# Moving the last LN1 tile, the reciprocal's spread and the later LN2 tiles in a fused attention and mixer kernel

## The chip, the core and the metric

The kernel runs on one core of one Trainium2 chip. A core has five engines that run at the same time and meet through semaphores: TensorE (PE in the profile; its weight loads are PEld), VectorE (DVE), ScalarE (ACT), GpSimd (POOL) and SyncE (SP), which in this kernel issues nearly all the transfers. Each engine takes its instructions in program order. The kernel fixes that order itself ("manual schedule"), so moving a line of Python moves an instruction in the queue of its engine.

The metric is device time in microseconds of the one core. The kernel before takes 265.07 us, the median of three runs (264.65 to 265.18). The profiled execution spans 264.0 us.

## The reference, cut to what matters

The input `x` has 2048 rows of 640 columns. Two branches are computed from it and mixed by a gate, row by row.

```python
g = sigmoid((x * gate_w).sum(-1))                 # one gate per row
# branch A: linear attention, 32 heads of 20 columns
q, k, v = split(x @ wqkv);  pq, pk = phi(q), phi(k)   # phi: t + 1 where t > 0, else exp(t), plus 1e-6
num = pq @ (pk^T v)                               # per head
den = pq . sum_over_rows(pk) + 1e-6               # one per row and head
a = (num / den) @ wo
# branch B: mixer and MLP
h  = gelu(layernorm(x) @ w1)                      # LN1
hs = row_shifted(h) @ w2                          # column groups shifted by +-1, +-2 rows
x1 = x + hs
b  = x1 + gelu(layernorm(x1) @ w3) @ w4           # LN2
out = g * a + (1 - g) * b
```

## The kernel before: the parts concerned

The 2048 rows are four tiles `t` of 512 rows, each of four chunks `cc` of 128 rows. `pair()` hands out one of four PSUM buffers in turn, each of two banks. `work` has four buffers for a normalized chunk `ln`, and `lnx_p` three for a transposed tile `lnxT`.

LayerNorm is applied on DVE and the result is transposed by a DMA, since the next product needs it with the columns on the partitions. LN1 of a chunk and LN2 of a chunk look alike; LN2 needs `x1`, which needs the product with `w2`:

```python
def ln1_apply(c):
    ...
    nc.vector.tensor_scalar(lnx[:], x_sb[:, c, 0:D], mv1[:, c, 0:1], rstd1[:, c:c + 1], ...)
    nc.sync.dma_start_transpose(lnxT[t][:, :, cc * P:(cc + 1) * P], lnx[:])

def w2_unit(t, cc):
    pt = pair()
    ...  # 10 matmuls
    nc.vector.tensor_tensor(x1, pt, x_sb, op=ALU.add)      # L431, frees the PSUM buffer
    ln_stats(...)                                           # two bn_stats, one bn_aggr (L290 to L292)

def ln2_apply(t, cc):
    ...
    nc.vector.tensor_scalar(ln[:], x1, mean, rstd, ...)     # L445; rstd is made on POOL (L286, L287)
    nc.sync.dma_start_transpose(st[t]["lnT"][:, :, cc * P:(cc + 1) * P], ln[:])   # L447
```

The denominators of the attention come out of PSUM, are inverted and spread over four tiles; four DMAs then copy them to the partitions where `pqT` has its rows, and `scale_t` multiplies `pqT` by them:

```python
def den_evac(pt):
    nc.vector.tensor_scalar_add(d, pt[:, 0, :], 1e-6)       # L265
    nc.vector.reciprocal(r_bf[:], d)                        # L267
    for t in range(NT):
        nc.vector.tensor_copy(r4[:, t, :], r_bf[H * t:H * (t + 1), :])   # L269
    for i in range(4):
        nc.sync.dma_start(rb[bass.ds(i, H, 4), :, :], r4[:])             # L271

def scale_t(t):                                             # L275
    nc.vector.tensor_tensor(pqT tile t, pqT tile t, rb[:, t] broadcast, op=ALU.mult)
```

The order in which the units are emitted, from the first product with `w1` on (each call adds its instructions to the queues of its engines at that place):

```python
for fcs in w1_split: w1_unit(0, fcs)          # w1_unit(t, (4,)) also makes four DVE copies of hx (L360)
kv_unit()
w1_unit(1, w1_split[0])
den_evac(den_mm())
for g in range(3): m_unit(g)
for cc in range(CPT): ln1_apply(3 * CPT + cc)
w1_unit(1, w1_split[1]); m_unit(3); m_unit(4); w1_unit(1, w1_split[2]); m_unit(5)
...
for cc in range(CPT):                         # tile 0: LN2 chunk by chunk
    w2_unit(0, cc)
    ln2_rstd(0, cc, cc + 1)
    if cc >= 1: ln2_apply(0, cc - 1)
for fcs in w1_split:
    w1_unit(2, fcs)
    if fcs[0] == 0: ln2_apply(0, CPT - 1)
m_regroup()                                   # mst to DRAM (2 DMAs, L389), back as m_sb (6 DMAs, L393)
load w4                                       # L576 to L578, 2.2 MB
scale_t(0); scale_t(1)
for fcs in w1_split: w1_unit(3, fcs)
scale_t(2); scale_t(3)
for cc in range(CPT): x1_scale(0, cc)
for t in range(NT):                           # the main loop
    for i in range(NW3):                      # NW3 = 7
        w3_unit(t, i)                         # 10 matmuls (5 for i = 6), L475, read the transposed LN2 tile t
        if i < CPT and t + 1 < NT: w2_unit(t + 1, i)        # L428
        if 2 <= i < 2 + CPT: att_unit(t, i - 2)             # 10 matmuls L459; DVE L462 adds into x1
    if t + 1 < NT:
        ln2_rstd(t + 1, 0, CPT)
        for cc in range(CPT): ln2_apply(t + 1, cc)
    if t == 0: w3_rest(0, ...)
    w4_tile(t)   # 52 matmuls L508, 8 matmuls L517, w3_rest(t + 1): 10 matmuls L483, 52 matmuls L508
```

`w3_rest(t + 1)` (L483) multiplies the last 64 columns of `w3` with the transposed LN2 tile `t + 1`. It is the first reader of that tile.

Of the kernel before, what the change touches and what calls it, by code (L numbers as in the profile page):

```python
# [16 lines left out]
def kernel(  # L17
# [20 lines left out]
    NT = S // TS  # L38
    CPT = TS // P
# [31 lines left out]
    def pair():  # L71
        return ps.tile([P, 2, 512], F32, name="pp")
# [182 lines left out]
    def den_mm():  # L255
        pt = pair()
        for j in range(DC):
            for t in range(NT):
                nc.tensor.matmul(pt[32 * t:32 * (t + 1), 0, :], lhsT=zbd[:, j, :], rhs=pqT[:, j, t * TS:(t + 1) * TS],
                                 start=(j == 0), stop=(j == DC - 1))  # L260
        return pt

    def den_evac(pt):
        d = e_p.tile([P, 1024], BF16, name="e")[:].bitcast(F32)
        nc.vector.tensor_scalar_add(d, pt[:, 0, :], 1e-6)  # L265
        with nc.allow_low_precision(reason="rounded after a float32 division, as a copy would"):
            nc.vector.reciprocal(r_bf[:], d)  # L267
        for t in range(NT):
            nc.vector.tensor_copy(r4[:, t, :], r_bf[H * t:H * (t + 1), :])  # L269
        for i in range(4):  # L270
            nc.sync.dma_start(rb[bass.ds(i, H, 4), :, :], r4[:])  # L271
# [13 lines left out]
    def rsqrt(out_ap, var_ap):  # L285
        nc.gpsimd.tensor_scalar_add(out_ap, var_ap, EPS)  # L286
        nc.gpsimd.tensor_tensor(out_ap, out_ap, mhalf[:, 0:out_ap.shape[1]], op=ALU.pow)  # L287

    def ln_stats(mv_ap, src_ap, st):
        nc.vector.bn_stats(st[:, 0, :], src_ap[:, 0:HD])  # L290
        nc.vector.bn_stats(st[:, 1, :], src_ap[:, HD:D])
        nc.vector.bn_aggr(mv_ap, st)  # L292
# [8 lines left out]
    def ln1_apply(c):  # L301
        t, cc = divmod(c, CPT)
        if cc == 0:
            lnxT[t] = lnx_p.tile([P, DC, TS], BF16, name="lnxT")
        lnx = work.tile([P, D], BF16, name="ln")
        nc.vector.tensor_scalar(lnx[:], x_sb[:, c, 0:D], mv1[:, c, 0:1], rstd1[:, c:c + 1],
                                op0=ALU.subtract, op1=ALU.mult)
        nc.sync.dma_start_transpose(lnxT[t][:, :, cc * P:(cc + 1) * P], lnx[:])
# [36 lines left out]
    def w1_unit(t, fcs):  # L345
        pt = pair()
        for i, fc in enumerate(fcs):
            for dc in range(DC):
                w = w1_sb[:, dc, CG * fc:CG * fc + P] if fc < 4 else w1x[:, dc, :]
                nc.tensor.matmul(pt[:, i, :], lhsT=w, rhs=lnxT[t][:, dc, :], start=(dc == 0), stop=(dc == DC - 1))  # L350
        for i, fc in enumerate(fcs):
            if fc < 4:
                o = 2 + shifts[fc] + t * TS
                nc.scalar.activation(hsT[:, fc, o:o + TS], pt[:, i, :], ACT.Gelu_apprx_tanh)
            else:
                hx = hx_p.tile([P, TS], BF16, name="hx")
                nc.scalar.activation(hx[:], pt[:, i, :], ACT.Gelu_apprx_tanh)
                for g in range(4):
                    o = 2 + shifts[g] + t * TS
                    nc.vector.tensor_copy(hsT[32 * g:32 * (g + 1), 4, o:o + TS], hx[32 * g:32 * (g + 1), :])  # L360
# [19 lines left out]
    def m_unit(g):  # L380
        pt = pair()
        for hf in range(2):
            nc.tensor.matmul(pt[:, hf, 0:HD], lhsT=kvT[:, row0[g]:row0[g] + P],  # L383
                             rhs=wo_sb[:, g, hf * HD:(hf + 1) * HD], start=True, stop=True)
        nc.scalar.copy(mst[:, g, :].rearrange("p (h e) -> p h e", h=2), pt[:, :, 0:HD])

    def m_regroup():
        for g in (0, 3):
            nc.sync.dma_start(m_dram[g:g + 3].rearrange("g p e -> p g e"), mst[:, g:g + 3, :])  # L389
        for g in range(NG):  # L390
            n = 4 * heads[g]
            p0 = P - DC * n if g == 5 else 0
            nc.sync.dma_start(m_sb[4 * head0[g]:4 * head0[g] + n, :, :],  # L393
                              m_dram[g, p0:p0 + DC * n, :].rearrange("(j r) e -> r j e", j=DC))
# [4 lines left out]
        w1_unit(0, fcs)  # L399
    kv_unit()  # L400
    w1_unit(1, w1_split[0])
    den_evac(den_mm())
    for g in range(3):
        m_unit(g)
    for cc in range(CPT):
        ln1_apply(3 * CPT + cc)
    w1_unit(1, w1_split[1])
    for g in range(3, 5):
        m_unit(g)
    w1_unit(1, w1_split[2])  # L410
    m_unit(5)
    s1.close()
    w4p = ctx.enter_context(tc.tile_pool(name="w4p", bufs=1))
    w4_sb = w4p.tile([P, FF + 1, D], BF16)
# [6 lines left out]
    def w2_unit(t, cc):  # L421
        c = t * CPT + cc
        if cc == 0:
            st[t] = dict(x1=[], mv=small.tile([P, CPT, 2], F32, name="mv2"))
        pt = pair()
        for hf in range(2):
            for fc in range(DC):
                nc.tensor.matmul(pt[:, hf, 0:HD], lhsT=hsT[:, fc, 2 + c * P:2 + (c + 1) * P],  # L428
                                 rhs=w2_sb[:, fc, hf * HD:(hf + 1) * HD], start=(fc == 0), stop=(fc == DC - 1))
        x1 = x1p.tile([P, D], F32, name="x1")  # L430
        nc.vector.tensor_tensor(x1[:].rearrange("p (h e) -> p h e", h=2), pt[:, :, 0:HD],  # L431
                                x_sb[:, c, 0:D].rearrange("p (h e) -> p h e", h=2), op=ALU.add)
        ln_stats(st[t]["mv"][:, cc, :], x1[:], small.tile([P, 2, 6], F32, name="bnst")[:])
        st[t]["x1"].append(x1)

    def ln2_rstd(t, c0, c1):
        if c0 == 0:
            st[t]["rstd"] = small.tile([P, CPT], F32, name="rstd2")
        rsqrt(st[t]["rstd"][:, c0:c1], st[t]["mv"][:, c0:c1, 1])

    def ln2_apply(t, cc):
        if cc == 0:
            st[t]["lnT"] = lnx_p.tile([P, DC, TS], BF16, name="lnxT")
        ln = work.tile([P, D], BF16, name="ln")
        nc.vector.tensor_scalar(ln[:], st[t]["x1"][cc][:], st[t]["mv"][:, cc, 0:1], st[t]["rstd"][:, cc:cc + 1],  # L445
                                op0=ALU.subtract, op1=ALU.mult)
        nc.sync.dma_start_transpose(st[t]["lnT"][:, :, cc * P:(cc + 1) * P], ln[:])  # L447
# [6 lines left out]
    def att_unit(t, cc):  # L454
        c = t * CPT + cc
        pt = pair()
        for hf in range(2):
            for j in range(DC):
                nc.tensor.matmul(pt[:, hf, 0:HD], lhsT=pqT[:, j, c * P:(c + 1) * P],  # L459
                                 rhs=m_sb[:, j, hf * HD:(hf + 1) * HD], start=(j == 0), stop=(j == DC - 1))  # L460
        x1 = st[t]["x1"][cc][:].rearrange("p (h e) -> p h e", h=2)
        nc.vector.scalar_tensor_tensor(x1, pt[:, :, 0:HD], gate[:, c:c + 1], x1, op0=ALU.mult, op1=ALU.add)  # L462
# [3 lines left out]
    def w3_unit(t, i):  # L466
        if i == 0:
            st[t]["h2"] = h2p.tile([P, FF * TS], BF16, name="h2")
        h2, lnT = st[t]["h2"], st[t]["lnT"]
        pt = pair()  # L470
        n = min(2, FF - 2 * i)
        for k in range(n):
            fc = 2 * i + k
            for dc in range(DC):
                nc.tensor.matmul(pt[:, k, :], lhsT=w3_sb[:, dc, fc * P:(fc + 1) * P], rhs=lnT[:, dc, :],  # L475
                                 start=(dc == 0), stop=(dc == DC - 1))
        nc.scalar.activation(h2[:, 2 * i * TS:(2 * i + n) * TS], pt[:].rearrange("p h e -> p (h e)")[:, 0:n * TS],  # L477
                             ACT.Gelu_apprx_tanh)
# [92 lines left out]
    for fcs in w1_split:  # L571
        w1_unit(2, fcs)
        if fcs[0] == 0:
            ln2_apply(0, CPT - 1)
    m_regroup()
    nc.sync.dma_start(w4_sb[:, 0:FF, :], B_w4[0:FF * P, :].rearrange("(c p) f -> p c f", p=P))  # L576
    nc.sync.dma_start(w4_sb[0:FR, FF, :], B_w4[FF * P:F, :])
    nc.sync.dma_start(w4_sb[FR:P, FF, :], B_w4[FF * P:F, :])  # L578
# [9 lines left out]
    for t in range(NT):  # L588
        for i in range(NW3):
            w3_unit(t, i)  # L590
            if i < CPT and t + 1 < NT:
                w2_unit(t + 1, i)
            if 2 <= i < 2 + CPT:
                att_unit(t, i - 2)
        if t + 1 < NT:
            ln2_rstd(t + 1, 0, CPT)
            for cc in range(CPT):
                ln2_apply(t + 1, cc)
        if t == 0:
            w3_rest(0, pair()[:, 0, 0:LT])  # L600
        w4_tile(t)
# [30 lines left out]
```

## Time and profile before

| engine | busy us | share of the span |
|---|---|---|
| PE (matmul) | 258.5 | 98% |
| PEld (weight load) | 159.1 | 60% |
| DVE | 142.4 | 54% |
| ACT | 83.2 | 32% |
| POOL | 18.5 | 7% |

A matmul on 512 columns is listed with a mean of 379 ns (L475); since matmuls overlap, ten of them take 2.16 us in the chain of work. The page also counts 1670 matmuls and a granted TensorE clock of 1.00 over the whole span. The DMA engines move 25.78 MB.

How to read it: the group view gives for each line, engine and operation the busy time, the mean of one instruction and the idle time just before it with what ended that idle time. The wait view sums who waited for whom. The timeline gives the start, the length and the count of merged instructions in order of time; its square brackets hold the idle time before them. "SPq" is SyncE's queue, where a DMA's row is only its issue and not its transfer.

### The profile page before, as it was taken

To read this page: it belongs to the slowest core of one execution; us is meant where nothing else is said; L and a number is where in the kernel's file an instruction comes from. 1 tells how busy PE (TensorE), PEld (TensorE's weight loads), DVE (VectorE), ACT (ScalarE), POOL (GpSimd) and SP (SyncE) were. 2 spreads that over 40 slices of the span, in tenths; PEclk is the share of its full clock that TensorE was granted. 3 is DMA by queue.
4 is the path that set the end of the run, shared out by engine and by line. 5 is a ranking of instruction groups with operands and counts; after the bars stand their busy time and mean duration, and the time that the engine had idled before them with its cause. 6 is when DMAs were issued, how large, how long until landed. Compare 5 with 4: busy or idle time off the path is not lost.

```text
span 264.0 us, 4139 instructions
## 1 busy us (share of the span) xinstructions
PE 258.5 (98%) x1670; PEld 159.1 (60%) x1670; DVE 142.4 (54%) x277; ACT 83.2 (32%) x124; POOL 18.5 (7%) x64
## 2 busy tenths in 40 slices
PE   7999999999999998999999999999999999999995
PEld 3777555688754643555567565567565577555553
DVE  1688778799947988955403455413356233112132
ACT  1455454321165347422502222412131332142200
POOL 3000040012220031001000001000000100000000
PEclk9999999999999999999999999999999999999999
DMA  7999987016672576990132000061100052100011
GB/s 191 187 198 379 364 246 292 0 27 124 124 98 55 109 100 179 194 310 15 25 77 75 25 2 0 0 102 51 48 2 0 0 85 68 52 0 0 0 52 50
DMA packets 47265, 25.78 MB, mean 98 GB/s; under 512 B 35214, under 2 KB 46478, under 8 KB 47246
## 3 DMA queue, kind: packets, MB, share of 16 engines
q1 hardware_dynamic: 46804, 25.03, 39.1%
q10 hardware_dynamic: 442, 0.49, 0.5%
q8 instruction: 13, 0.21, 0.3%
q14 instruction: 6, 0.05, 0.1%
HBM read 13.03 MB, written 3.60 MB: 63 GB/s over the span
## 4 chain that ended last, share of the span: by engine, by line
PE 84%; DMA 7%; DVE 4%; SPq 3%; issue 1%; POOL 0%; DVEq 0%
PE pp L475 21%; PE pp L508 16%; PE pp L316 8%; PE pp L459 8%; PE pp L244 8%; PE pp L187 8%; PE pp L428 7%; DMA lnxT<-ln 5%; PE pp L350 4%; DVE ln L445 2%; SPq L447 2%; DMA wk_sb<-in_A_wqkv_dram 2%; PE pp L483 1%; PE pp L383 1%; DVE x L431 1%
## 5 line engine op out<-in xcount | busy, mean ns | idle before, releaser
L475 PE MATMUL pp<-lnxT,w_sb 128*128 128x512 bf16 x260 | 60.4, 379 | 0.9 <-DMA lnxT<-ln 0.9
L508 PE MATMUL pp<-w_sb,h 128*128 128x384 bf16 (+3 forms) x416 | 57.9, 299 | 0.0
L477 ACT ACTIVATE h<-pp 128x1024 bf16<-128x1024 f32 (+1 forms) x28 | 26.9, 962 | 83.2 <-PE pp L475 83.2
L508 PEld LDWEIGHTS <-h 128*128 128x128 bf16 x416 | 38.3, 98 | 19.3 <-issue 1.1
L475 PEld LDWEIGHTS <-w_sb 128*128 128x128 bf16 x260 | 25.4, 98 | 27.9 <-issue 1.3
L522 DVE SCALAR_TENSOR_TENSOR oc<-pp,omg,x 128x640 bf16<-128x640 f32 (+2 forms) x20 | 14.4, 748 | 45.9 <-ACT h2x L486 22.1
L462 DVE SCALAR_TENSOR_TENSOR x<-pp,gate,x 128x640 f32<-128x640 f32 x16 | 13.9, 867 | 29.4 <-PE pp L459 29.4
L179 ACT ACTIVATE e<-pp 128x640 bf16<-128x640 f32 (+1 forms) x26 | 21.5, 827 | 9.6 <-PE pp L244 9.6
L459 PE MATMUL pp<-m_sb,pqT 128*128 128x320 bf16 x160 | 24.3, 299 | 0.0
L428 PE MATMUL pp<-w_sb,hsT 128*128 128x320 bf16 x160 | 23.9, 299 | 0.0
L431 DVE TENSOR_TENSOR x<-pp,x_sb 128x640 f32<-128x640 f32 x16 | 13.1, 820 | 19.4 <-PE pp L428 19.3
L187 PE MATMUL pp<-wk_sb,xT 128*128 128x320 bf16 (+1 forms) x160 | 22.6, 299 | 0.9 <-DMA wk_sb<-in_A_wqkv_dram 0.7
L316 PE MATMUL pp<-x_sb,pk 128*128 128x320 bf16 (+1 forms) x160 | 22.0, 300 | 0.0
L244 PE MATMUL pp<-xT,hsT 128*128 128x512 bf16 x100 | 21.7, 379 | 0.0
L316 PEld LDWEIGHTS <-pk 128*128 128x128 bf16 x160 | 18.8, 117 | 3.2
L428 PEld LDWEIGHTS <-hsT 128*128 128x128 bf16 x160 | 15.7, 98 | 8.0
L459 PEld LDWEIGHTS <-pqT 128*128 128x128 bf16 x160 | 15.7, 98 | 7.7
L187 PEld LDWEIGHTS <-xT 128*128 128x128 bf16 x160 | 15.7, 98 | 7.4 <-issue 1.1
L350 PE MATMUL pp<-lnxT,w_sb 128*128 128x512 bf16 x80 | 18.1, 379 | 0.0
L244 PEld LDWEIGHTS <-hsT 128*128 128x128 bf16 x100 | 11.8, 118 | 9.7
L286 POOL TENSOR_SCALAR rstd<-mv 128x4 f32<-128x4 f32 (+1 forms) x11 | 3.2, 290 | 155.6 <-DVE mv L292 155.6
L181 DVE SCALAR_TENSOR_TENSOR pk<-pp,e 128x640 bf16<-128x640 f32 x16 | 13.2, 824 | 1.7
(75 smaller groups left out, 187.8 us busy)
## 6 DMA issues: line engine op xcount, KB each, us to landing
out_dram<-oc SPq DMA_DIRECT2D x14, 160.0 KB, 1.8
w_sb<-in_B_w_dram SPq DMA_DIRECT2D x1, 2160.0 KB
w_sb<-in_B_w_dram SPq DMA_DIRECT2D x1, 2080.0 KB, 11.9
x_sb<-in_A_x_dram SPq DMA_DIRECT2D x1, 1280.0 KB
x_sb<-in_A_x_dram SPq DMA_DIRECT2D x1, 960.0 KB, 7.4
wo_sb<-in_A_wo_dram SPq DMA_DIRECT2D x6, 160.0 KB, 7.8
m_dram<-mst SPq DMA_DIRECT2D x2, 480.0 KB, 3.0
hsT<-in_A_wqkv_dram SPq DMA_DIRECT2D x1, 800.0 KB
```

Source lines behind the costliest of these rows:

```text
L179: nc.scalar.activation(ev, src, ACT.Exp)
L187: nc.tensor.matmul(pt[:, hf, 0:n], lhsT=xT[:, dc, c * P:(c + 1) * P], rhs=wk_sb[:, dc, hf * HD:hf * HD + n], start=(dc == first), stop=(dc ...
L244: nc.tensor.matmul(pt[:, t % 2, :], lhsT=wq_sb[:, dc, :].rearrange("p (m j) -> p j m", j=DC)[:, j], rhs=xT[:, dc, t * TS:(t + 1) * TS], st ...
L316: nc.tensor.matmul(pt[:, hf, 0:HD + hf], lhsT=w, rhs=x_sb[:, c, hf * HD:(hf + 1) * HD + hf], start=(c == 0), stop=(c == NCH - 1))
L350: nc.tensor.matmul(pt[:, i, :], lhsT=w, rhs=lnxT[t][:, dc, :], start=(dc == 0), stop=(dc == DC - 1))
L428: nc.tensor.matmul(pt[:, hf, 0:HD], lhsT=hsT[:, fc, 2 + c * P:2 + (c + 1) * P], rhs=w2_sb[:, fc, hf * HD:(hf + 1) * HD], start=(fc == 0), ...
L431: nc.vector.tensor_tensor(x1[:].rearrange("p (h e) -> p h e", h=2), pt[:, :, 0:HD], x_sb[:, c, 0:D].rearrange("p (h e) -> p h e", h=2), op ...
L459: nc.tensor.matmul(pt[:, hf, 0:HD], lhsT=pqT[:, j, c * P:(c + 1) * P], rhs=m_sb[:, j, hf * HD:(hf + 1) * HD], start=(j == 0), stop=(j == D ...
L475: nc.tensor.matmul(pt[:, k, :], lhsT=w3_sb[:, dc, fc * P:(fc + 1) * P], rhs=lnT[:, dc, :], start=(dc == 0), stop=(dc == DC - 1))
L477: nc.scalar.activation(h2[:, 2 * i * TS:(2 * i + n) * TS], pt[:].rearrange("p h e -> p (h e)")[:, 0:n * TS], ACT.Gelu_apprx_tanh)
L508: nc.tensor.matmul(dst, lhsT=st[t]["h2"][:, fc * TS + cc * P:fc * TS + (cc + 1) * P], rhs=w4_sb[:, fc, a:b], start=start and fc == 0, stop ...
L522: nc.vector.scalar_tensor_tensor(oc[:, a:b], src, omg[:, c:c + 1], st[t]["x1"][cc][:, a:b], op0=ALU.mult, op1=ALU.add)
```

## The change

Three things move; no arithmetic is added or removed. First, `den_evac` is cut in three. The addition of 1e-6 stays where it was, then the four `ln1_apply` of the last LN1 tile come ahead of the reciprocal, and the spread (four DVE copies and four DMAs) goes behind the last `ln2_apply` of tile 0. Second, `m_regroup` is cut in two: the stores to DRAM go out as soon as the last `m_unit` is done, the loads stay where they were, now behind the spread. Third, in the main loop LN2 of the next tile is no longer applied after the seventh `w3_unit`. Its reciprocal root is taken right after the last `w2_unit` (i = 3), and two chunks are applied behind the second attention unit (i = 3) and two behind the third (i = 4). The aim is that the transposed tiles are ready when TensorE asks for them.

```diff
@@ den_evac
         d = e_p.tile([P, 1024], BF16, name="e")[:].bitcast(F32)
         nc.vector.tensor_scalar_add(d, pt[:, 0, :], 1e-6)
+        return d
+
+    def den_recip(d):
         with nc.allow_low_precision(reason="rounded after a float32 division, as a copy would"):
             nc.vector.reciprocal(r_bf[:], d)
+
+    def r_spread():
         for t in range(NT):
             nc.vector.tensor_copy(r4[:, t, :], r_bf[H * t:H * (t + 1), :])
         for i in range(4):
@@ m_regroup
-    def m_regroup():
+    def m_store():
         for g in (0, 3):
             nc.sync.dma_start(m_dram[g:g + 3].rearrange("g p e -> p g e"), mst[:, g:g + 3, :])
+
+    def m_load():
         for g in range(NG):
@@ emission
     w1_unit(1, w1_split[0])
-    den_evac(den_mm())
+    den = den_evac(den_mm())
+    for cc in range(CPT):
+        ln1_apply(3 * CPT + cc)
+    den_recip(den)
     for g in range(3):
         m_unit(g)
-    for cc in range(CPT):
-        ln1_apply(3 * CPT + cc)
     w1_unit(1, w1_split[1])
     for g in range(3, 5):
         m_unit(g)
     w1_unit(1, w1_split[2])
     m_unit(5)
+    m_store()
@@ behind LN2 of tile 0
         if fcs[0] == 0:
             ln2_apply(0, CPT - 1)
-    m_regroup()
+            r_spread()
+    m_load()
@@ main loop
             if i < CPT and t + 1 < NT:
                 w2_unit(t + 1, i)
+                if i == CPT - 1:
+                    ln2_rstd(t + 1, 0, CPT)
             if 2 <= i < 2 + CPT:
                 att_unit(t, i - 2)
-        if t + 1 < NT:
-            ln2_rstd(t + 1, 0, CPT)
-            for cc in range(CPT):
-                ln2_apply(t + 1, cc)
+            if i in (3, 4) and t + 1 < NT:
+                for cc in range(2 * i - 6, 2 * i - 4):
+                    ln2_apply(t + 1, cc)
```

TensorE, ScalarE and GpSimd keep their order of instructions; only the queues of DVE and SP are reordered.

## The prediction

> **What bounds the kernel now.** I read the page's table of engines first, then the waits of TensorE, then the timeline around each wait, and last the chain of waits for the landing times of transfers. Table of engines and waits (us in total, times, longest):
>
> ```profile
> PE 258.5 (98%) x1670; PEld 159.1 (60%) x1670; DVE 142.4 (54%) x277; ACT 83.2 (32%) x124; POOL 18.5 (7%) x64
> ...
> PE pp L475 <- DMA lnxT<-ln: 0.9, 1, 0.9
> PE pp L200 <- PEq L616: 0.8, 1, 0.8
> PE pp L187 <- DMA wk_sb<-in_A_wqkv_dram: 0.7, 1, 0.7
> ```
>
> TensorE has work for 258.5 of 264.0 us. Of the 5.5 us without, most lie at the two ends, which the change does not touch; inside the span there is one listed wait of its matmuls that the change addresses, 0.88 us at L475. So whatever DVE and SP gain, only a hole of TensorE can be turned into time. The timeline shows that hole and three stages of L483:
>
> ```profile
> 103.92 2.32 PE L475 MATMUL pp<-lnxT,w_sb 128*128 128x512 bf16 x10 [0.88 <-DMA lnxT<-ln]
> ...
> 137.40 1.14 PE L483 MATMUL pp<-lnxT,w_sb 128*64 128x256 bf16 x10
> ...
> 178.24 1.10 PE L483 MATMUL pp<-lnxT,w_sb 128*64 128x256 bf16 x10
> ...
> 219.05 0.74 PE L483 MATMUL pp<-lnxT,w_sb 128*64 128x256 bf16 x10
> ```
>
> The same ten L483 matmuls take 0.74 us in tile 2 but 1.14 and 1.10 us in tiles 0 and 1. The reader is to see that 0.40 and 0.36 us of "busy" are waiting: the first matmul's span holds it. L483's own listing gives the weight loads two waits on the transpose, 0.6 us together. The landings in the chain agree:
>
> ```profile
> 101.22 2.57 DMA lnxT<-ln
> ...
> 133.43 4.33 DMA lnxT<-ln
> 137.80 0.73 PE pp L483 x9
> ...
> 175.96 2.60 DMA lnxT<-ln
> ```
>
> The last transpose for tile 0 lands at 103.79, and for the next two tiles at 137.76 and 178.56, each time just after TensorE wants it.
>
> **What the Trainium skill says.** "Trainium Kernel Development and Optimization", Best Practices: matmul busy time is not the distance to the roofline, because matmuls are pipelined. The trace agrees: L483 reads busy while it waits, and PEld is busy only 60%. It is no reserve for this change, which leaves the matmuls as they are. "DMA: Bandwidth & Descriptors", Anatomy of one DMA, says that a semaphore wait is done by the issuing sequencer before dispatch. The wait view of SP agrees: L271, the spread, waited 5.8 us and held what stood behind it in the queue, the LN1 transposes. The same section gives about 2 us of fixed cost per DMA (for GpSimd's path), mostly the receipt. This trace has 1.8 us from issue to landing for the 160 KB stores and 2.57 us for the last transpose; I use 2.0 us for a 128 KB spread DMA, an estimate between them.
>
> **The change part by part, LN2 of tile 0.** The timeline of before:
>
> ```profile
> 82.56 3.35 DVE L267 RECIPROCAL r_bf<-e 128x512 bf16<-128x512 f32 x1
> ...
> 85.95 1.17 DVE L269 COPY r<-r_bf 32x512 bf16<-32x512 bf16 x4
> ...
> 87.15 1.52 DVE L306 TENSOR_SCALAR ln<-x_sb,mv,rstd 128x640 bf16<-128x640 bf16 x4
> ...
> 88.58 1.19 DVE L360 COPY hsT<-hx 32x512 bf16<-32x512 bf16 x4
> 89.75 5.94 SPq L308 DMA_TRANSPOSE lnxT<-ln  x4
> 89.80 0.82 DVE L431 TENSOR_TENSOR x<-pp,x_sb 128x640 f32<-128x640 f32 x1
> ...
> 94.43 0.61 DVE L445 TENSOR_SCALAR ln<-x,mv,rstd 128x640 bf16<-128x640 f32 x1 [0.79 <-DMA lnxT<-ln]
> ```
>
> After: the addition ends at 82.56, the four L306 (4 x 0.38) run to 84.1, the reciprocal to 87.4. The copies L360 need ACT's hx, ready at 87.70 (87.06 + 0.64), so they run 87.7 to 88.9, and the first L431 starts near 88.9 in place of 89.80: 0.9 us earlier. The second gain is the 0.79 us wait at L445. It is for a `work` buffer: LN2's first chunk takes the one of an LN1 chunk whose transpose was issued only at 89.75. Now that transpose is issued near 83 and lands long before. So LN2 of tile 0 runs about 0.9 + 0.79 = 1.7 us earlier: its last L445 ends near 99.5 (before: 100.58 + 0.61 = 101.19), and the last transpose lands near 99.5 + 2.57 = 102.1. TensorE is free for L475 at 103.92 - 0.88 = 103.04, a margin of about 1.0 us. The hole of 0.88 us goes. The product w1 of tile 2, which runs meanwhile, does not wait for DVE.
>
> **LN2 of the later tiles.** Before, four L445 of 2.17 us in all start at 128.81, after the last attention unit. In the new place the reciprocal root is ready near 123.0 (POOL L287 at 121.94, 1.04 long), two L445 run 123.0 to 124.1, in time for the third attention unit's L462 (it began at 124.49 after 2.19 us idle), two more run behind it, 125.4 to 126.5, before the fourth (128.01). DVE sits idle there, so nothing is displaced beyond a tenth. The transposes are issued about 4 us or more earlier; L483 finds its tile in both places, 0.40 + 0.36 = 0.76 us. Tile 2 has no hole and gains nothing.
>
> **The sum of the removed.** 0.88 + 0.40 + 0.36 = 1.64 us: 265.07 - 1.64 = 263.43 us.
>
> **What is pushed later: the spread.** Its cost is zero on DVE (the same 1.17 us of copies), but its landing moves, and `scale_t` stands behind it in DVE's queue. What follows there in before:
>
> ```profile
> 102.31 2.89 DVE L275 TENSOR_TENSOR pqT<-pqT,rb 128x2560 bf16<-128x2560 bf16 x2
> ...
> 105.12 1.19 DVE L360 COPY hsT<-hx 32x512 bf16<-32x512 bf16 x4
> ...
> 106.32 2.89 DVE L275 TENSOR_TENSOR pqT<-pqT,rb 128x2560 bf16<-128x2560 bf16 x2
> ...
> 109.13 0.82 DVE L431 TENSOR_TENSOR x<-pp,x_sb 128x640 f32<-128x640 f32 x1
> ...
> 113.11 1.52 PE L428 MATMUL pp<-w_sb,hsT 128*128 128x320 bf16 x10
> ```
>
> That L431 empties the PSUM buffer of the first `w2_unit(1, ...)`, and the third one (L428 at 113.11) is four `pair()` later: it takes the same buffer. From scale to the end of L431 DVE needs 109.95 - 102.31 = 7.64 us. After the change the copies L269 end near 99.5 + 1.2 = 100.7, four issues of 0.6 us follow, the last starting near 100.7 + 3 x 0.62 = 102.55, and it lands near 104.55. Then L431 ends near 104.55 + 7.64 = 112.2. TensorE, now 0.88 us earlier, wants the buffer at 113.11 - 0.88 = 112.23. The two meet: zero as computed, but each part of a microsecond that the spread lands later becomes a wait. With an uncertainty of some 0.8 us in the landing the mean wait is about 0.3 us; I put 0.2. The attention unit behind it has `m_sb` in time: the loads are now issued near 103.2, before at 105.53, since the stores went out early.
>
> **The rivals.** (1) The new wait eats the first gain. If the spread lands at 105.5 or later, L428 waits 0.9 us or more and only the 0.76 us at L483 remain: 264.3 us. For it speaks that the landing is my estimate and not in the trace; against it that the queue is otherwise empty then, so the four DMAs need share nothing. (2) The early transposes meet something new. DMA share over 1 at low GB/s near 78 to 79 and 92.5 to 93.5 us, and single transpose issues of 2 us and more, show that transposes can be held up by over 1 us. If one falls on the last transposes of tile 0, the hole of 0.88 us stays: again near 264.3. Against it: before, nothing of the kind lay between 97 and 103 us. The earlier DRAM stores (near 88.5 to 92) could hold up LN1's last transposes, but those are first read by w1 of tile 3 at 97.5. (3) LN2 between the attention units delays L462 and with it the PSUM buffers. DVE is idle 2.2 and 2.6 us before L462 there, against 0.7 us of waiting for POOL plus 1.1 us of work: it should fit; if not, some 0.3 us per tile come back. (4) A profile of TensorE as the bound that hides more waiting in its modelled ends than I found: then the gain could reach 2 us, 263.0.
>
> **Range and chances.** All outcomes lie between about 263.0 (all holes gone and a little more) and 264.6 (rival 1 or 2 and the spread of runs, 0.5 us before). Predicted 263.6 us, 1.5 us or 0.6% less than before; 8 in 10 for 263.0 to 264.6. A 2% gain would need 259.8 us, more than all of TensorE's idle time inside the span; a 2% loss 270.4, a wait of 5 us that no part of the change can make: 1 in 100 each, 98 in 100 within 2%.
>
> **What would show it right or wrong.** Right: no wait of PE at L475; three L483 stages of 0.74 us; the last L445 of tile 0 ending near 99.5; the first L431 near 88.9; L275 starting near 104.5. Wrong: a wait of PE at L428 or an idle row before the third `w2_unit(1, ...)` near 112 us, whose size is what I took for 0.2; a wait on L459 for `pqT` or `m_sb`; L462 late behind L445. I would be wrong altogether if TensorE's stages without a change (a main-loop tile, 24 us of L475, L428 and L459) became longer.

## The result and the profile after

The changed kernel takes 263.60 us (median of 6 runs, 263.32 to 263.66) against 265.12 us for the kernel before in the same comparison: a ratio of 0.9942, 95% interval 0.9924 to 0.9960. That is 1.5 us less. The profiled executions differ by more, 264.0 to 261.9 us. The one of the kernel before took 265.70 us of device time, 0.6 us over its median, and 0.32 us of the difference lies in the first 7 us: the steady run of the first product (L187) starts at 7.07 us before and at 6.75 us after. Nothing there was changed. Times of before and after below can be compared by adding these 0.32 us to those of after.

The line numbers of the changed kernel are shifted: L475 became L484 (w3), L483 became L492 (the rest of w3), L428 became L437 (w2), L431 became L440 (the DVE addition behind w2), L445 became L454 (LN2), L459 became L468 (attention), L275 became L280 (`scale_t`), L350 became L355 (w1).

Of the changed kernel, the table of engines and the waits of TensorE (us in total, times, longest), then its timeline at the same four places as shown of before (start, length, instructions merged, idle time before in brackets):

```profile
PE 256.3 (98%) x1651; PEld 158.7 (61%) x1670; DVE 142.2 (54%) x277; ACT 82.9 (32%) x124; POOL 18.7 (7%) x64
...
PE pp L200 <- PEq L627: 0.8, 1, 0.8
PE pp L187 <- DMA wk_sb<-in_A_wqkv_dram: 0.6, 2, 0.4
PE pp L187 <- DVE wk_sb L223: 0.2, 1, 0.2
PE pp L517 <- issue: 0.2, 1, 0.2
```

```profile
101.48 1.24 PE L355 MATMUL pp<-lnxT,w1x 128*128 128x512 bf16 x5
...
102.56 2.32 PE L484 MATMUL pp<-lnxT,w_sb 128*128 128x512 bf16 x9
...
136.03 0.74 PE L492 MATMUL pp<-lnxT,w_sb 128*64 128x256 bf16 x10
...
176.48 0.74 PE L492 MATMUL pp<-lnxT,w_sb 128*64 128x256 bf16 x10
...
216.93 0.74 PE L492 MATMUL pp<-lnxT,w_sb 128*64 128x256 bf16 x10
```

In the kernel before, the last w1 unit began here:

```profile
101.80 1.24 PE L350 MATMUL pp<-lnxT,w1x 128*128 128x512 bf16 x5
```

TensorE's program is the same in both kernels; where a row says x9 for ten matmuls, and the table 1651 for 1670, records are missing from the trace. The reader is to see three things. No wait on a transposed tile is left. The first w3 unit starts 1.08 us after the last w1 unit began (101.48), where before it took 2.12 us (101.80 to 103.92): 1.04 us gained. And the rest of w3 takes 0.74 us in every tile, where tiles 0 and 1 took 1.14 and 1.10: 0.76 us gained. The sum is 1.80 us; the two profiles differ by 2.1 - 0.32 = 1.78 us. So the whole difference lies in these three holes, and no new one has opened: from the first w3 unit to the rest of w3 of tile 0 it is 33.48 us before (103.92 to 137.40) and 33.47 us after, and from there to the rest of w3 of tile 1 it is 40.84 us before, of which 0.40 us is the hole, and 40.45 us after.

### The profile page after: what moved, and what is told of

It is laid out like the page before. It is cut to its first block, busy times and chain, and to the rows that moved or that the text cites. A ratio compares the mean times of both kernels' runs of the same rounds, so it can differ in the third digit from the quotient of the medians.

```text
span 261.9 us, 4122 instructions
## 1 busy us (share of the span) xinstructions
PE 256.3 (98%) x1651; PEld 158.7 (61%) x1670; DVE 142.2 (54%) x277; ACT 82.9 (32%) x124; POOL 18.7 (7%) x64
## 4 chain that ended last, share of the span: by engine, by line
PE 96%; DMA 2%; issue 1%; SPq 0%; DVE 0%
PE pp L517 22%; PE pp L484 21%; PE pp L321 8%; PE pp L437 8%; PE pp L468 8%; PE pp L244 8%; PE pp L355 8%; PE pp L187 8%; DMA wk_sb<-in_A_wqkv_dram 2%; PE pp L492 1%; PE pp L526 1%; PE pp L388 1%; PE pp L374 1%; PE pp L259 0%; SPq L127 0%
## 5 line engine op out<-in xcount | busy, mean ns | idle before, releaser
L484 PE MATMUL pp<-lnxT,w_sb 128*128 128x512 bf16 x249 | 59.8, 379 | 0.6
L484 PEld LDWEIGHTS <-w_sb 128*128 128x128 bf16 x260 | 25.4, 98 | 26.8
L468 PE MATMUL pp<-m_sb,pqT 128*128 128x320 bf16 x160 | 24.3, 299 | 0.0
L437 PE MATMUL pp<-w_sb,hsT 128*128 128x320 bf16 x160 | 23.9, 299 | 0.0
L187 PE MATMUL pp<-wk_sb,xT 128*128 128x320 bf16 (+1 forms) x160 | 22.6, 299 | 0.9 <-DMA wk_sb<-in_A_wqkv_dram 0.6
L440 DVE TENSOR_TENSOR x<-pp,x_sb 128x640 f32<-128x640 f32 x16 | 13.0, 812 | 15.7 <-PE pp L437 15.7
L437 PEld LDWEIGHTS <-hsT 128*128 128x128 bf16 x160 | 15.7, 98 | 8.0
L468 PEld LDWEIGHTS <-pqT 128*128 128x128 bf16 x160 | 15.7, 98 | 7.7
L187 PEld LDWEIGHTS <-xT 128*128 128x128 bf16 x160 | 15.6, 98 | 7.2 <-issue 0.9
L355 PE MATMUL pp<-lnxT,w_sb 128*128 128x512 bf16 x77 | 17.9, 379 | 0.2
```

What stands on the lines that cost most here:

```text
L187: nc.tensor.matmul(pt[:, hf, 0:n], lhsT=xT[:, dc, c * P:(c + 1) * P], rhs=wk_sb[:, dc, hf * HD:hf * HD + n], start=(dc == first), stop=(dc ...
```

## Experiments

All ratios are to the kernel before, run beside on the same chip.

**The loop alone.** The last hunk of the change, on the kernel before: `ln2_rstd` behind the last `w2_unit`, two `ln2_apply` each behind i = 3 and i = 4, nothing else.

> Only the later LN2 tiles are moved between the attention units; everything about tile 0 is as before. Theory (each part closes its own hole of TensorE): the ten L483-kind matmuls take 0.74 us in all three tiles (before 1.14, 1.10, 0.74), the wait of 0.88 us ahead of the first w3 unit stays, and the time falls by 0.76 us to about 264.3. Rival (only the tile 0 part matters, and LN2 in the loop displaces the attention's additions): 265.1 or more.

Measured: 264.39 us, ratio 0.9975 (0.9961 to 0.9989), 0.72 us less. Its timeline:

```profile
103.06 2.32 PE L475 MATMUL pp<-lnxT,w_sb 128*128 128x512 bf16 x10 [0.75 <-DMA lnxT<-ln]
...
136.54 0.74 PE L483 MATMUL pp<-lnxT,w_sb 128*64 128x256 bf16 x10
...
176.98 0.74 PE L483 MATMUL pp<-lnxT,w_sb 128*64 128x256 bf16 x10
```

The two later holes are closed and the first stays. The rival falls.

**Tile 0 alone.** The change without its last hunk.

> Only the tile 0 part (LN1 ahead of the reciprocal, late spread, early stores); the loop is as before. Theory: the wait ahead of the first w3 unit is gone (0.9 to 1.0 us), the L483-kind stages stay at 1.1 us in tiles 0 and 1, time about 264.1; with the first experiment the two gains add up to the whole. Rival (the late spread gives the gain back at the w2 units of tile 1): 265.0.

Measured: 264.41 us, ratio 0.9980 (0.9966 to 0.9995), 0.70 us less where 0.9 to 1.0 was expected. The timeline says why:

```profile
102.12 2.32 PE L484 MATMUL pp<-lnxT,w_sb 128*128 128x512 bf16 x10
...
135.72 1.10 PE L492 MATMUL pp<-lnxT,w_sb 128*64 128x256 bf16 x10
...
176.53 0.84 PE L492 MATMUL pp<-lnxT,w_sb 128*64 128x256 bf16 x10
...
217.08 0.30 PE L492 MATMUL pp<-lnxT,w_sb 128*64 128x256 bf16 x1
217.72 0.73 PE L492 MATMUL pp<-lnxT,w_sb 128*64 128x256 bf16 x9 [0.35 <-DMA lnxT<-ln]
218.39 3.81 PE L517 MATMUL pp<-w_sb,h 128*128 128x256 bf16 x27
```

The first hole is gone, but the holes of the loop are not a fixed price: tile 1 has 0.10 us where before had 0.36, and tile 2, which had none, loses 0.64. The bracket shows only 0.35 of these. The first of the ten matmuls reads only the first two chunks of the tile, so it starts before the last transpose has landed, and its 0.30 us cover a part of the wait. What is lost is seen from the start of the first matmul to the start of what follows: 217.08 to 218.39 is 1.31 us, and without a hole it is 0.67 us (219.05 to 219.72 in tile 2 of the kernel before). By this count the loop's holes are 0.36 + 0.10 + 0.64 = 1.10 us here and 0.76 us in the kernel before. The first attention unit also starts 0.12 us late (112.79; the third w2 unit began at 111.31 and takes 1.36). So the traces have 1.04 us of gain less 0.34 (1.10 - 0.76) less 0.12, or 0.58 us, near the 0.70 us measured. The wait at the w2 units of tile 1 that the rival expected is not there. While LN2 stays at the end of the loop, its last transpose lands within some tenths of being wanted in every tile. The two parts together, 0.72 + 0.70 = 1.42 us, make the whole of the change within its uncertainty.

**The turn of the PSUM buffers.** I had said that the third `w2_unit(1, .)` takes the buffer of the first. In the changed profile that cannot be: it starts at 111.75, and the addition which empties the first one's buffer runs from 112.15 to 112.97. The built programs give the reason. Which of the four buffers `pair()` returns is not a fixed turn, as I had taken it to be; it is settled when the program is built, and it changed:

```
unit             w3(0,0) w2(1,0) w3(0,1) w2(1,1) w3(0,2) w2(1,2) att(0,0)
kernel before       1       2       3       0       1       2       3
changed kernel      2       1       0       3       2       0       1
```

Two kernels have the turn written out, one with that of before, one with its own:

```diff
-    ps = ctx.enter_context(tc.tile_pool(name="ps", bufs=4, space=PSUM))
+    ps = [ctx.enter_context(tc.tile_pool(name=f"ps{k}", bufs=1, space=PSUM)) for k in range(4)]
     def pair():
-        return ps.tile([P, 2, 512], F32, name="pp")
+        return ps[int(next(turn_of))].tile([P, 2, 512], F32, name="pp")   # turn_of: the 131 numbers
```

> The changed kernel, with the turn in which the four PSUM buffers are handed out fixed to that of the kernel before: the third w2_unit(1, .) shares its buffer with the first, whose DVE addition ended at 112.97 in the changed kernel while TensorE began the third unit at 111.75. Theory (the late spread does delay DVE, and only the new turn of the buffers hides it): TensorE waits about 1.2 us there and the time is about 264.8. Rival (the delay of DVE does not matter in either turn): 263.6.

> The changed kernel with its own turn of the PSUM buffers written out in the same way: the control of the experiment beside it. Both theories: 263.6, no wait of TensorE near 112 us.

Measured: with the old turn 264.93 us, ratio 1.0000 (0.9984 to 1.0017); with its own turn 263.45 us, ratio 0.9944 (0.9928 to 0.9960). The old turn costs 1.48 us and gives back the whole gain. The timeline of the old turn:

```profile
111.83 0.81 DVE L442 TENSOR_TENSOR x<-pp,x_sb 128x640 f32<-128x640 f32 x1
...
112.70 1.52 PE L439 MATMUL pp<-w_sb,hsT 128*128 128x320 bf16 x10 [1.25 <-DVE x L442]
```

TensorE waits 1.25 us for the addition that the late spread has held up. The kernel with its own turn has no such line:

```profile
111.45 1.52 PE L439 MATMUL pp<-w_sb,hsT 128*128 128x320 bf16 x10
...
112.04 0.82 DVE L442 TENSOR_TENSOR x<-pp,x_sb 128x640 f32<-128x640 f32 x1
...
112.91 1.52 PE L470 MATMUL pp<-m_sb,pqT 128*128 128x320 bf16 x10
```

The rival falls: the delay of DVE is real and the new turn hides it, though not with room to spare. In the new turn the first attention unit (L470) takes the buffer that this addition empties at 112.86, and it starts 0.10 us later than the 1.36 us of the w2 unit would let it.

**LN1 first, and nothing else.** The four `ln1_apply` moved ahead of the reciprocal; the spread stays right behind it, the loop and the stores as before.

```diff
         nc.vector.tensor_scalar_add(d, pt[:, 0, :], 1e-6)
+        for cc in range(CPT):
+            ln1_apply(3 * CPT + cc)
         ... reciprocal, four copies, four DMAs
-    for cc in range(CPT):
-        ln1_apply(3 * CPT + cc)
```

> The kernel before with one move alone: the four LN1 applications of the last tile ahead of the reciprocal, the spread still right behind the reciprocal, all else as before. Theory (of the hole of 0.88 us, 0.79 us is LN2's wait for a work buffer, which the early LN1 transposes free; the first DVE addition of w2 stays where it was since the same work lies ahead of it): no wait of DVE at the first LN2, a hole of about 0.1 us left, time about 264.3. Rival (the 0.9 us of the spread's copies must leave the path too): about half of the hole stays, 264.7.

Measured: 264.80 us, ratio 0.9994 (0.9977 to 1.0011). By its time this is inconclusive, and the expected 264.3 was missed. Its timeline:

```profile
93.30 0.57 DVE L445 TENSOR_SCALAR ln<-x,mv,rstd 128x640 bf16<-128x640 f32 x1
...
101.68 1.24 PE L352 MATMUL pp<-lnxT,w1x 128*128 128x512 bf16 x5
102.76 2.32 PE L475 MATMUL pp<-lnxT,w_sb 128*128 128x512 bf16 x10
...
136.23 1.11 PE L483 MATMUL pp<-lnxT,w_sb 128*64 128x256 bf16 x10
...
217.50 0.30 PE L483 MATMUL pp<-lnxT,w_sb 128*64 128x256 bf16 x1
218.19 0.73 PE L483 MATMUL pp<-lnxT,w_sb 128*64 128x256 bf16 x9 [0.40 <-DMA lnxT<-ln]
218.86 3.38 PE L508 MATMUL pp<-w_sb,h 128*128 128x256 bf16 x24
```

LN2's first chunk no longer waits and the hole ahead of the first w3 unit is gone (101.68 to 102.76 is 1.08 us), as the theory has it and against the rival. Of the loop's holes, counted from the first matmul to what follows, this execution has 0.38 us in tile 0 and 0.69 us in tile 2: 1.07 us, where the kernel before has 0.76. So in this execution a part of what is gained at tile 0 is lost again in the loop, as in the one traced of tile 0 alone. The executions of this kernel lie between 263.73 and 266.57 us; whether this explains its median as a whole was not settled.

**Six `work` buffers.** The kernel before, `bufs=4` to `bufs=6` in the pool of `ln`, no instruction moved.

> The kernel before with six work buffers in place of four, no instruction moved. Theory (the 0.79 us ahead of the first LN2 is a wait for a buffer, not for data): that wait of DVE is gone, the hole of TensorE falls from 0.88 to about 0.1 us, time about 264.3. Rival (the wait is really for something else that lands at the same moment, or the transposes of LN2 then queue behind those of LN1 and land no earlier): 265.1.

Measured: 264.17 us, ratio 0.9973 (0.9957 to 0.9988), 0.87 us less. The timeline shows LN2's first chunk without a wait, and the last w1 unit began at 101.42, so the w3 unit follows after 1.21 us where 1.08 is without a hole:

```profile
93.17 0.58 DVE L445 TENSOR_SCALAR ln<-x,mv,rstd 128x640 bf16<-128x640 f32 x1
...
101.42 1.24 PE L350 MATMUL pp<-lnxT,w1x 128*128 128x512 bf16 x5
...
102.63 2.32 PE L475 MATMUL pp<-lnxT,w_sb 128*128 128x512 bf16 x10
```

So the 0.79 us wait was for a buffer, and two more buffers do nearly all that moving LN1 does at this place. The loop's holes, counted as above, are only 0.23 us in this execution, all in tile 0 (136.10 to 137.00, less 0.67), where LN1 first had 1.07: with LN2 at the end of the loop they differ from one execution to the next, and most of the distance between the traces of these two kernels lies there. In the built program the turn of the PSUM buffers changed here too (2, 0, 1, 3, 2, 0, 1 for the seven units above), though only the size of another pool was edited; the third w2 unit still shares its buffer with the first, and no wait is seen there.

**Early spread with the loop's part.** The kernel of "LN1 first" with the loop's hunk; the stores still late.

> The move of the third experiment of this list's first entry together with the main loop's part of the change; the spread stays early, so scale_t need not wait for it. Theory: DVE has no wait for the spread, no wait of TensorE near 112 us in any turn of the buffers, a hole of at most 0.1 us ahead of the first w3 unit, three L483-kind stages of 0.74 us: 263.5 to 263.7, the same as the changed kernel. Rival (the late spread is what makes the whole gain possible): 264.0 to 264.4.

Measured: 263.39 us, ratio 0.9940 (0.9921 to 0.9960). The late spread is not needed for the gain. The first w3 unit starts 1.08 us after the last w1 unit began (101.12 to 102.20), and all three stages of L483 take 0.74 us.

```profile
111.39 1.52 PE L428 MATMUL pp<-w_sb,hsT 128*128 128x320 bf16 x10
112.89 1.52 PE L459 MATMUL pp<-m_sb,pqT 128*128 128x320 bf16 x10
```

Between the end of the third w2 unit (its ten matmuls take 1.36 us in the chain) and the first attention unit 0.14 us are left, which the next two experiments explain.

**Late stores.** The changed kernel with the two stores of `m_store` behind the spread again, just ahead of the loads.

> The changed kernel with the two stores to DRAM moved back behind the spread, ahead of their loads. Theory (m_sb is wanted only near 113 us, so the early stores are worth nothing): the loads are issued near 106 us, land near 110, TensorE does not wait, 263.6. Rival (the loads come too late, or delay the w4 load): a wait at the first attention unit and 264 or more.

Measured: 265.10 us, ratio 1.0009 (0.9996 to 1.0022): I was wrong and the rival right. The timeline:

```profile
107.13 2.40 SPq L400 DMA_DIRECT2D m_sb<-m_dram  x6
...
112.50 1.52 PE L436 MATMUL pp<-w_sb,hsT 128*128 128x320 bf16 x10
...
115.25 1.52 PE L467 MATMUL pp<-m_sb,pqT 128*128 128x320 bf16 x10 [1.23 <-DMA m_sb<-m_dram]
```

The loads wait for the stores, are issued from 107.13 to 109.53 and are there only at 115.2, not near 110. The first attention unit waits for them: 1.23 us in the bracket, 1.39 us from the end of the third w2 unit (112.50 + 1.36). The early stores are what makes the late spread affordable on the SP queue.

**All early.** Early spread, early stores and the loop's part, beside the changed kernel itself.

> The early spread and the main loop's part together with the early stores to DRAM. Theory: the 0.14 us that TensorE waited ahead of the first attention unit with late stores is gone, DVE has no wait for the spread, TensorE has no hole left between its first and last w4 unit: 0.1 to 0.2 us under the same kernel with late stores, and level with the changed kernel beside it (263.3 to 263.6), since no hole of TensorE is left to close there either. Rival (the changed kernel still hides waiting that the early spread frees): 0.3 us or more under the changed kernel.

> The changed kernel itself beside it on the same chip: 263.5 to 263.7 by either theory.

Measured: 263.40 us, ratio 0.9939 (0.9920 to 0.9958), and for the changed kernel 263.43 us, ratio 0.9941 (0.9923 to 0.9959). The two are level, and the rival falls. The 0.1 to 0.2 us expected under the same kernel with late stores (263.39 us, on another chip) is not seen in the time, only in the timeline:

```profile
100.72 2.89 DVE L277 TENSOR_TENSOR pqT<-pqT,rb 128x2560 bf16<-128x2560 bf16 x2
...
107.55 0.82 DVE L434 TENSOR_TENSOR x<-pp,x_sb 128x640 f32<-128x640 f32 x1
...
111.54 1.52 PE L431 MATMUL pp<-w_sb,hsT 128*128 128x320 bf16 x10
112.90 1.52 PE L462 MATMUL pp<-m_sb,pqT 128*128 128x320 bf16 x10
```

Here the third w2 unit does share its buffer with the first, and the addition is over at 108.37, 3.2 us ahead. The attention unit follows without the 0.14 us. No version was found that beats the changed kernel. This one only has more slack, because it does not rest on who shares a buffer with whom.

## Why the prediction came out right, point by point

**TensorE as the bound: right.** Every gain seen is a closed hole of TensorE; versions in which DVE has less to wait for, but TensorE has no hole, are level.

**LN2 of tile 0, 1.7 us earlier: right.** The DVE steps came at the times worked out:

```profile
88.64 0.82 DVE L440 TENSOR_TENSOR x<-pp,x_sb 128x640 f32<-128x640 f32 x1
...
92.40 0.57 DVE L454 TENSOR_SCALAR ln<-x,mv,rstd 128x640 bf16<-128x640 f32 x1
...
98.50 0.61 DVE L454 TENSOR_SCALAR ln<-x,mv,rstd 128x640 bf16<-128x640 f32 x1 [0.77 <-POOL rstd L292]
```

With 0.32 us added, the first addition is at 88.96 (predicted 88.9) and the last LN2 ends at 99.43 (99.5). The 0.79 us as a buffer wait is shown by the six buffers. The hole was 1.04 us in place of 0.88: the listed wait does not hold all of it. One reading on the way was off: the 5.8 us that the spread waited in SyncE's queue did not hold up the LN1 transposes, since their rows were only made from 87.15 us on, when that wait was over. What held them was DVE's order, with the reciprocal and the copies ahead, and then the 2.49 us of the four issues (87.15 to 89.64).

**The loop's 0.76 us: right in sum,** as three stages of 0.74 us and the loop alone (0.72 us) show. That tile 2 "has no hole" was luck of that execution: with LN2 at the end of the loop it lost 0.64 and 0.69 us in two other traces.

**The late spread, 0.2 us: the number was near, the step was not.** Two terms were wrong and cancelled. First the landing. The changed kernel's DMA view (KB each, us to landing) and timeline:

```profile
rb<-r SPq DMA_DIRECT2D x4, 128.0 KB, 2.7
```

```profile
105.33 2.89 DVE L280 TENSOR_TENSOR pqT<-pqT,rb 128x2560 bf16<-128x2560 bf16 x2 [3.91 <-DMA rb<-r]
...
111.75 1.52 PE L437 MATMUL pp<-w_sb,hsT 128*128 128x320 bf16 x10
...
112.15 0.82 DVE L440 TENSOR_TENSOR x<-pp,x_sb 128x640 f32<-128x640 f32 x1
...
113.11 1.52 PE L468 MATMUL pp<-m_sb,pqT 128*128 128x320 bf16 x10
```

I took 2.0 us, which is also about the fixed cost of a DMA that the Trainium skill gives for the GpSimd path ("DMA: Bandwidth & Descriptors", Anatomy of one DMA). Here, issued from SyncE, it is 2.7 us, and `scale_t` starts at 105.33 + 0.32 = 105.65, not 104.55: 1.1 us late, 0.7 us of it in the landing. What makes the landing take 2.7 us stays open. The condition of rival 1 (105.5 or later) was met. Second, "it takes the same buffer" failed: in the changed program it takes another one, and the wait of 1.25 us that the old turn shows is not paid. The one that now takes the first unit's buffer is the first attention unit at 113.11, 0.14 us after the addition ends at 112.97. In the traces of tile 0 alone and of the control with its own turn TensorE came some tenths earlier, and that unit did start 0.12 and 0.10 us late. That the predicted 263.6 us was met was therefore luck: with this landing and the sharing I had assumed, the gain is gone, as the old turn shows with 264.93 us.

**The stores: right, and worth more than I thought later.** The prediction had `m_sb` in time because the stores went out early; I then expected nothing of moving them back, having sized the landing of the loads some 5 us too short.

**Rivals 2 and 3 did not come true.** The transposes of LN2 were issued in 1.20 to 1.35 us each in the changed kernel, and the attention's additions began when TensorE had finished. Rival 4 holds in small: the first hole was 0.16 us more than the listed wait.

## What to carry to other kernels

When one engine is busy 98% of the time, look for its holes, also inside rows that read as busy, by comparing equal groups of instructions in different stages; close each and count only that. Count a hole from the start of one group to the start of the next, since a wait that the profile lists can be less than what is lost (0.35 of 0.64 us here). A wait that is listed for a transfer can be a wait for a buffer of the pool, and two more buffers can then do what a reordering does. Where a pool hands out buffers when the program is built, a reordering of one engine also changes who shares a buffer with whom: read the sharing from the built program of each version, since it decided over 1.48 us here.

## What the hardware showed that I had not expected

A 128 KB DMA between partitions took 2.7 us to land, a store of 160 KB 1.8 us. With late stores the six `m_sb` loads landed about 5.7 us after the last was issued (109.53 to 115.25), with the 2.2 MB load of w4 issued right behind them; whether that load held them up was not tried. And a transpose of the same shape landed after 2.57, 2.60 or 4.33 us in the kernel before. In the case of 4.33 us the DMA engines had been quiet, but for a few packets, since 135.6 us, 2.2 us before the landing at 137.76, and in that of 2.60 us since 178.1 us, 0.5 us before it. So the longer one was not longer for the data; its cause stays open too.
